# Second MLP's output GEMM by seven products instead of eight, with copied banks and stored input sums

## The chip, the cores and the metric

The kernel runs on one core of a Trainium2 chip. The metric is the device time of one execution in microseconds (us), the median of several runs. TensorE (PE) multiplies, VectorE (DVE) and ScalarE (ACT) do the elementwise work, GpSimd (POOL) and SyncE (SP) mostly issue DMAs. SBUF is the on-chip memory, PSUM the eight banks into which PE accumulates.

## What is computed

```
x = attention(q, k, v)          # keys and values averaged over 8 positions; 4608 tokens x 512
h = x @ w_in;  g = min(relu(0.5 h + 0.5)^2, 1) max h;  y = g @ w_out           # first MLP, 2048 wide
out = (sigmoid(y @ w_gate) * (y @ w_val)) @ w_out2                              # second MLP, 1536 wide
```

All in fp32. Each fp32 operand is split into a high part (fp32r, a cast) and a low part (the value minus the high part), and a product is three matmuls: high by high, high by low, low by high (`three`, L578 to L582).

## The kernel before, in words

Tokens are worked on in nine blocks of 512. The first MLP takes the nine blocks in turn; the attention of the next block runs between its matmuls. The second MLP takes block 0 alone (L797 to L826) and then four pairs of blocks (L829 to L937). A pair has a gate stage: six steps i, in each n = 0 (gate) and n = 1 (value), and for each of these twelve a 2 x 2 block product of weights (256 x 512) with inputs (512 x 1024) by Strassen's scheme in Winograd's form, seven products (`product`, L882) of six matmuls 128x512 each instead of eight. Two blocks of the seven weight matrices come from sums that block 0 computes and writes to DRAM (`prepare`, L730); a pair loads all seven of one (i, n) in one DMA of 1792 KB (`load_seven`, L765) into one of three buffers (`wa`, `wa`, `wb`). The input sums T1 to T4 are computed at the start of each pair (L852 to L870: four subtractions `minus` and seven splits for each of two halves).

Products land in four PSUM banks A to D; DVE adds (`add`, L890) combine them with SBUF copies, and `finish` (L897) applies the sigmoid or multiplies. The result `gs` (24 of 128x512 a pair) is the left operand of the output GEMM (`out_part`, L779): for each of two blocks, twelve steps m of twelve matmuls, each step split on ACT (L781) and DVE (L782), against weights that stay in SBUF (`w2`, twelve `win` buffers). `out_rows` (L592) copies the four accumulator banks out and stores.

The order on every engine is made at build time. Each operation has an engine, a cost and a key, which is a due time; `Plan.issue` (L132) walks a model of the engines and takes, among operations that could start at nearly the same time, the one with the lowest key. Keys are no earliest times: an operation goes as soon as its data and buffers are there. On the chip each engine follows the resulting order and waits on semaphores. SP's DMAs are issued in one order too.

Of the kernel before, what the change touches and what calls it, by code (L numbers as in the profile page):

```python
# [8 lines left out]
F32 = mybir.dt.float32  # L9
# [9 lines left out]
P = 128  # L19
# [45 lines left out]
class Plan:  # L65
# [7 lines left out]
    def op(self, eng, cost, key, fn, r=(), w=(), after=(), behind=(), nbytes=0, share=1.0, dmas=1):  # L73
# [24 lines left out]
        o.data, o.order = data, order - data  # L98
# [98 lines left out]
def pooled_attention_two_mlps(  # L197
# [46 lines left out]
    one, att, two = ExitStack(), ExitStack(), ExitStack()  # L244
# [50 lines left out]
    def due2(j, m):  # L295
        return due1(NB * M1 + 2) + S2 * (j * M2 + m)
# [372 lines left out]

    pools2 = {}  # L670

    def second_a():
        att.close()
        pools2["wa"] = two.enter_context(tc.tile_pool(name="wa", bufs=2))

    def second_b():
        one.close()
        pools2["right"] = two.enter_context(tc.tile_pool(name="two", bufs=1, side="right"))

    open_a = op("none", 0.0, 0.0, second_a, behind=att_ops)  # L680
    open_b = op("none", 0.0, 0.0, second_b, behind=one_ops)

    def late(tag, bufs, shape, dtype=F32, fifo=True):

        b = Buf(lambda: pools2["wa" if tag == "wa" else "right"], tag, bufs, shape, dtype, fifo)
        b.behind = [open_a if tag == "wa" else open_b]
        return b
# [5 lines left out]
    def buf_win(behind):  # L693
        b = Buf(win_p, "win", M1, [P, 2, TB], F32R)
        b.behind = behind
        return b
# [12 lines left out]
    PSTEP = 11 * 2.6  # L709
# [55 lines left out]
    def load_seven(n, i, key):  # L765
        sl, d = buf_seven(), seven[2 * i + n]
        op2(SP, 0.475, key, lambda: nc.sync.dma_start(
            out=sl.t.rearrange("p s k f -> p (s k f)").bitcast(F32), in_=d.t), r=[d], w=[sl], nbytes=P * 2 * NMAT * HK * 4)
        return sl
# [9 lines left out]
    def out_part(gs, m, key, accs, last, ahead=5):  # L779
        g = buf_g()  # L780
        op2(ACT, 0.62, key - ahead, lambda: nc.scalar.copy(out=g.t[:, 0], in_=gs.t), r=[gs], w=[g])  # L781
        op2(DVE, 0.69, key - ahead + 1, lambda: nc.vector.tensor_tensor(  # L782
            out=g.t[:, 1], in0=gs.t, in1=g.t[:, 0].bitcast(F32), op=ALU.subtract), r=[gs, g], w=[g])
# [6 lines left out]

    def buf_gs():
        return late("gs", 12, [P, TB], fifo=False)
# [9 lines left out]
    accs = [bank("acc") for _ in range(4)]  # L802
    for i in range(MP):
        slots = [prepare(n, i, due2(0, 2 * i) - 6 + 2.6 * n) for n in range(2)]
        T = due2(0, 2 * i)
        banks = {(n, f): bank("ha"[n], True) for n in range(2) for f in range(2)}
        for n in range(2):
            sl, a21 = slots[n]
            for f in range(2):
                last = []  # L810
                for c in range(KD):
# [5 lines left out]
                    last = [op(PE, 0.65, T + 5.2 * n + 2.6 * f + 0.1 * c, mm, r=[sl, a21, xs[c]], w=[banks[n, f]], behind=last)]  # L817
        for f in range(2):
            m = 2 * i + f
            t, gs = Buf(t_p, "t", 2, [P, TB]), buf_gs()  # L820
            op(ACT, 0.6, T + 2.6 * f + 5, lambda t=t, pg=banks[0, f]: nc.scalar.activation(out=t.t, in_=pg.t, func=AF.Sigmoid),
               r=[banks[0, f]], w=[t])
            op2(DVE, 0.69, T + 2.6 * f + 6, lambda t=t, gs=gs, pv=banks[1, f]: nc.vector.tensor_tensor(
                out=gs.t, in0=pv.t, in1=t.t, op=ALU.mult), r=[t, banks[1, f]], w=[gs])
            out_part(gs, m, due2(0, m) + 2 * S2 + 5.2, accs, lasts)
    out_rows(due2(0, M2 + 1) + 6, out[0:TB, :], accs)  # L826


    for pr in range(NPR):  # L829
        j1, j2 = 1 + 2 * pr, 2 + 2 * pr  # L830
        T0p = PAIR0 + PSTEP * MP * pr
        Tx = T0p - 4
# [19 lines left out]
        for kt in range(2):  # L852
            x_raw(B11[kt], 1, j1, kt, Tx - 20 + 0.1 * kt)
        for kt in range(2):
            x_raw(B22[kt], 0, j2, kt, Tx - 19 + 0.1 * kt)
            x_raw(B22[kt], 1, j2, 2 + kt, Tx - 19 + 0.1 * kt)
        for kt in range(2):
            x_raw(T4[kt], 1, j1, 2 + kt, Tx - 18 + 0.1 * kt)
        for kt in range(2):
            b11, t1, t2, t3, t4, b22 = (x[kt] for x in (B11, T1, T2, T3, T4, B22))  # L860
            u1 = minus(lambda b=b22: b.t[:, 0], lambda b=b11: b.t[:, 1], Tx + 0.1 * kt, [b22, b11])
            x_split(b11, Tx + 1 + 0.1 * kt)
            u2 = minus(lambda b=b22: b.t[:, 1], lambda b=u1: b.t, Tx + 2 + 0.1 * kt, [b22, u1])
            split_u(u1, t1, Tx + 7 + 0.1 * kt)
            u4 = minus(lambda b=t4: b.t[:, 1], lambda b=u2: b.t, Tx + 3 + 0.1 * kt, [t4, u2])
            split_u(u2, t2, Tx + 4 + 0.1 * kt)
            split_u(u4, t4, Tx + 9 + 0.1 * kt)
            u3 = minus(lambda b=b22: b.t[:, 1], lambda b=b22: b.t[:, 0], Tx + 5 + 0.1 * kt, [b22])
            split_u(u3, t3, Tx + 6 + 0.1 * kt)
            x_raw(B21[kt], 1, j1, 2 + kt, Tx - 17 + 0.1 * kt)  # L870
            x_split(B21[kt], Tx + 8 + 0.1 * kt)
            x_split(b22, Tx + 10 + 0.1 * kt)

        gss = {}
        for i in range(MP):
            sig = {}
            for n in range(2):
                T = T0p + PSTEP * i + PSTEP / 2 * n
                H = PSTEP / 14
                sl = load_seven(n, i, T - 24)  # L880

                def product(pos, o, mat, xx, start, sl=sl):  # L882
                    def mm():
                        for k in range(2):
                            ks = slice(k * P, k * P + P)
                            three(o.t, sl.t[:, 0, mat, ks], sl.t[:, 1, mat, ks], xx[k].t[:, 0], xx[k].t[:, 1],
                                  start and k == 0, k == 1, not start)
                    op(PE, 1.3, T + H * pos, mm, r=[sl] + xx + ([] if start else [o]), w=[o])
# [8 lines left out]
                def finish(key, fi, b, u):  # L897
# [7 lines left out]
                    else:  # L905
                        s, g = sig[fi], buf_gs()
                        gss[fi[1], 2 * i + fi[0]] = g
                        if u:
                            add(key, g, b, u)
                        op2(DVE, 0.69, key + 0.5, lambda: nc.vector.tensor_tensor(  # L910
                            out=g.t, in0=(g if u else b).t, in1=s.t, op=ALU.mult), r=[s, g] if u else [s, b], w=[g])

                A, Bk, Ck, Dk = bank("h", True), bank("a", True), bank("h", True), bank("a", True)
                s1 = Buf(f_p, "f", 3, [P, TB])
                u2, u3 = (late("u", 3, [P, TB]) for _ in range(2))
# [4 lines left out]
                product(2, Ck, 5, T3, True)  # L920
                add(T + H * 3, u3, Ck, u2)
                product(3, Dk, 3, T1, True)
                finish(T + H * 4, (1, 1), Dk, u3)
                product(4, A, 1, B21, False)
                finish(T + H * 5, (0, 0), A, None)
                product(5, Ck, 2, T4, False)
                finish(T + H * 6, (1, 0), Ck, u2)
                product(6, Dk, 6, B22, False)
                finish(T + H * 7, (0, 1), Dk, u2)

        for b in range(2):
            accs = [bank("acc") for _ in range(4)]
            for m in range(M2):
                out_part(gss[b, m], m, T0p + PSTEP * (3.4 + (M2 * b + m) / 4), accs, lasts, 40)
            j = j1 + b
            out_rows(T0p + PSTEP * (3.4 + (M2 * b + M2) / 4) + 1, out[j * TB:(j + 1) * TB, :], accs)

# [32 lines left out]
```

## Time and profile before

| | |
|---|---|
| median of 3 runs | 1756.0 us (1752.55 to 1757.51) |
| the profiled execution | 1755.67 us, of which the traced span is 1753.8 us |
| PE busy | 1723.8 us, 98% of the span |
| DVE busy | 1051.5 us, 60% |
| ACT busy | 805.7 us, 46% |
| DMA | 234.37 MB, mean 134 GB/s |

Busy is time in which an engine has an instruction in work; PE's matmuls are pipelined, so each is recorded as 389 ns while the next starts 227 ns after it. A wait is named after what ended it. "PEclk" is the TensorE clock granted, as a share of full speed. DMA share is the time of the packets as a share of sixteen DMA engines; packets that overlap can bring it above 1.

### The profile page before, as it was taken

To read this page: it belongs to the slowest core of one execution; us is meant where nothing else is said; L and a number is where in the kernel's file an instruction comes from. 1 tells how busy PE (TensorE), PEld (TensorE's weight loads), DVE (VectorE), ACT (ScalarE), POOL (GpSimd) and SP (SyncE) were. 2 spreads that over 40 slices of the span, in tenths; PEclk is the share of its full clock that TensorE was granted. 3 is DMA by queue.
4 is the path that set the end of the run, shared out by engine and by line. 5 is a ranking of instruction groups with operands and counts; after the bars stand their busy time and mean duration, and the time that the engine had idled before them with its cause. 6 is when DMAs were issued, how large, how long until landed. Compare 5 with 4: busy or idle time off the path is not lost.

```text
span 1753.8 us, 24039 instructions
## 1 busy us (share of the span) xinstructions
PE 1723.8 (98%) x9016; PEld 1393.4 (79%) x9016; DVE 1051.5 (60%) x1874; ACT 805.7 (46%) x1786; POOL 52.7 (3%) x90
## 2 busy tenths in 40 slices
PE   7899999999999999999999999999999999999998
PEld 5676777778777778777887888888888888888887
DVE  5899867677776867574646645345444644464432
ACT  5876656566665656564755332123222312141212
POOL 0000001010010101010000000000000000000000
PEclk9999999999999999999999999999999999999999
DMA  7742525243443414031415875354344433443411
GB/s 205 229 119 69 149 57 163 62 134 97 116 116 92 134 45 134 16 128 40 174 39 202 318 291 204 126 192 145 126 146 166 149 119 146 166 167 126 150 43 49
DMA packets 148532, 234.37 MB, mean 134 GB/s; under 512 B 84160, under 2 KB 104640, under 8 KB 140736
## 3 DMA queue, kind: packets, MB, share of 16 engines
q1 hardware_dynamic: 138624, 182.50, 33.1%
q0 software_dynamic: 9792, 50.34, 7.9%
q8 instruction: 71, 1.16, 0.3%
q14 instruction: 45, 0.37, 0.1%
HBM read 173.02 MB, written 50.33 MB: 127 GB/s over the span
## 4 chain that ended last, share of the span: by engine, by line
PE 92%; DMA 3%; DVE 2%; ACT 1%; SPq 0%; issue 0%; DVEq 0%; ACTq 0%
PE acc L580 13%; PE h L580 13%; PE acc L582 13%; PE acc L581 13%; PE h L582 13%; PE h L581 12%; PE a L582 4%; PE a L581 4%; PE a L580 4%; PE a L484 2%; DMA raw<-in_moe_w_out_dram 1%; PE a L413 1%; DMA kv<-in_v_dram 1%; DMA x<-in_v_dram 1%; DMA xb<-y 0%
## 5 line engine op out<-in xcount | busy, mean ns | idle before, releaser
L580 PE MATMUL h<-x,win 128*128 128x512 f32 x576 | 231.2, 401 | 1.0 <-ACT win L505 1.0
L580 PE MATMUL acc<-g,wj 128*128 128x512 f32 x576 | 228.7, 397 | 1.2 <-ACT g L505 1.2
L582 PE MATMUL acc<-g,wj 128*128 128x512 f32 x576 | 225.4, 391 | 3.5 <-DVE wj L514 3.5
L582 PE MATMUL h<-x,win 128*128 128x512 f32 x576 | 225.7, 392 | 1.3 <-DVE win L514 1.3
L581 PE MATMUL acc<-g,wj 128*128 128x512 f32 x576 | 225.6, 392 | 1.0 <-DVE g L514 1.0
L581 PE MATMUL h<-x,win 128*128 128x512 f32 x576 | 225.5, 391 | 0.0
L781 ACT CAST g<-gs 128x512 fp32r<-128x512 f32 x108 | 66.8, 622 | 319.2 <-PE acc L582 200.4
L645 ACT ACTIVATE t<-h,half 128x512 f32<-128x512 f32 x144 | 99.2, 689 | 186.9 <-PE h L582 186.9
L582 PE MATMUL acc<-win,g 128*128 128x512 f32 x432 | 168.2, 389 | 2.1 <-DVE g L782 2.1
L580 PE MATMUL acc<-win,g 128*128 128x512 f32 x432 | 168.2, 389 | 0.0
L581 PE MATMUL acc<-win,g 128*128 128x512 f32 x432 | 168.1, 389 | 0.0
L782 DVE TENSOR_TENSOR g<-gs,g 128x512 fp32r<-128x512 f32 x108 | 74.1, 690 | 135.2 <-ACT g L781 135.0
L649 DVE SCALAR_TENSOR_TENSOR t<-t,h 128x512 f32<-128x512 f32 x144 | 97.3, 676 | 90.9 <-ACT t L647 90.8
L580 PEld LDWEIGHTS h<-x,win 128*128 128x128 f32 x576 | 108.7, 189 | 35.7 <-issue 9.7
L582 PEld LDWEIGHTS acc<-g,wj 128*128 128x128 f32 x576 | 108.4, 188 | 28.4 <-DVE wj L514 5.4
L580 PEld LDWEIGHTS acc<-g,wj 128*128 128x128 f32 x576 | 108.2, 188 | 27.8 <-ACT g L505 1.7
L582 PEld LDWEIGHTS h<-x,win 128*128 128x128 f32 x576 | 108.7, 189 | 25.9 <-DVE win L514 2.5
L581 PEld LDWEIGHTS acc<-g,wj 128*128 128x128 f32 x576 | 108.3, 188 | 23.2 <-DVE g L514 1.6
L581 PEld LDWEIGHTS h<-x,win 128*128 128x128 f32 x576 | 108.8, 189 | 21.1
L514 DVE TENSOR_TENSOR wj<-wout_f,wj 128x512 fp32r<-128x512 f32 x144 | 99.0, 688 | 33.3 <-ACT wj L505 33.0
L514 DVE TENSOR_TENSOR g<-t,g 128x512 fp32r<-128x512 f32 x144 | 98.8, 686 | 33.6 <-ACT g L505 33.1
L505 ACT CAST g<-t 128x512 fp32r<-128x512 f32 x144 | 89.1, 619 | 52.5 <-DVE t L649 50.1
(212 smaller groups left out, 3231.1 us busy)
## 6 DMA issues: line engine op xcount, KB each, us to landing
wa<-seven SPq DMA_DIRECT2D x32, 1792.0 KB
wb<-seven SPq DMA_DIRECT2D x16, 1792.0 KB
seven<-wa POOLq DMA_DIRECT2D x8, 1792.0 KB, 7.4
y<-raw SPq DMA_DIRECT2D x18, 512.0 KB
w<-f POOLq DMA_DIRECT2D x36, 256.0 KB, 2.5
out_dram<-raw SPq DMA_DIRECT2D x18, 512.0 KB
win<-in_moe_w_in_dram SPq DMA_DIRECT2D x16, 512.0 KB
raw<-in_moe_w_out_dram SPq DMA_DIRECT2D x16, 512.0 KB
```

Source lines behind the costliest of these rows:

```text
L413: nc.tensor.matmul(out=scs[h].t[r0 % P:r0 % P + D, r0 // P * C:r0 // P * C + C], lhsT=qT.t[D * h:D * h + D, r0:r0 + D], rhs=kts[b % 2, p]. ...
L484: nc.tensor.matmul(out=px.t[D * h:D * h + D, lo:hi], lhsT=vps[b % 2, p].t[:, h], rhs=rhs, start=True, stop=True)
L505: ACT: (0.52, lambda: nc.scalar.copy(out=dst.t[:, 0], in_=src())),
L514: op(engs, [0.6 if e == DVE else 1.23 for e in engs], key, [lambda e=e: by[e].tensor_tensor(out=dst.t[:, 1], in0=src(), in1=dst.t[:, 0].bi ...
L580: nc.tensor.matmul(out=o, lhsT=wh, rhs=xh, start=start, stop=False, skip_group_check=more)
L581: nc.tensor.matmul(out=o, lhsT=wh, rhs=xl, start=False, stop=False, skip_group_check=more)
L582: nc.tensor.matmul(out=o, lhsT=wl, rhs=xh, start=False, stop=stop, skip_group_check=more)
L645: op(ACT, 0.69, Tg, lambda t=t, hps=hps: nc.scalar.activation(out=t.t, in_=hps.t, func=AF.Relu, bias=half.t, scale=0.5), r=[hps, half], w=[t])
L649: op(DVE, 0.69, Tg + 2, lambda t=t, hps=hps: nc.vector.scalar_tensor_tensor(out=t.t, in0=t.t, scalar=1.0, in1=hps.t, op0=ALU.min, op1=ALU. ...
L781: op2(ACT, 0.62, key - ahead, lambda: nc.scalar.copy(out=g.t[:, 0], in_=gs.t), r=[gs], w=[g])
L782: op2(DVE, 0.69, key - ahead + 1, lambda: nc.vector.tensor_tensor(out=g.t[:, 1], in0=gs.t, in1=g.t[:, 0].bitcast(F32), op=ALU.subtract), r ...
```

## The change

The output GEMM of each pair becomes a 2 x 2 block product as well: `hs[i]` holds, for step i, the rows f = 0, 1 of both blocks (two buffers of 128 x 2 x 512), and `out_pair` runs seven products of six steps with six matmuls each, 252 matmuls instead of 288. `prepare_out` makes the seven output weight matrices of each i in pair 0 and writes them to DRAM (42 DMAs of 256 KB from POOL); every product step loads its 256 KB back, into five `wo` buffers. The sums of the left operand are formed in place in `hs` (`comb`, four for each i). Results come out transposed: DVE transposes 32x32 blocks and SP stores runs of 256 B (`store`); the very last quarter is turned on PE (`store_rows`). In the gate stage one DMA for each product (256 KB, runs of 1 KB in DRAM, nine `ws` buffers) takes the place of the 1792 KB load, and ACT copies one bank into another before a product accumulates on it (`to_bank`), in place of DVE adds. The input sums of pairs 1 to 3 are formed during the pair before (`input_sums`, after steps 2 and 4), written to DRAM and loaded back. The new pools are opened once all of block 0's weight slots are done with (`open_c`).

```diff
-    PSTEP = 11 * 2.6
+    PSTEP = 10.5 * 2.6
...
-    def load_seven(n, i, key):
-        sl, d = buf_seven(), seven[2 * i + n]
+    def load_seven(n, i, mat, key):
+        w, d = late("ws", 9, [P, 2, HK], F32R), seven[2 * i + n]
         op2(SP, 0.475, key, lambda: nc.sync.dma_start(
-            out=sl.t.rearrange("p s k f -> p (s k f)").bitcast(F32), in_=d.t), r=[d], w=[sl], nbytes=P * 2 * NMAT * HK * 4)
+            out=w.t.bitcast(F32), in_=d.t.rearrange("p (s k f) -> p s k f", s=2, k=NMAT)[:, :, mat]), r=[d], w=[w], nbytes=P * 2 * HK * 4)
...
+    open_c = op("none", 0.0, 0.0, second_c, behind=[u for x in wb_slots for u in x.users])
...
+    def prepare_out(i, key):
+        a = Buf(raw_p, "raw", 2, [P, 4, HK], fifo=False)
+        sm = late("o", 2, [P, 4, HK])
...
+        comb(0, lambda: a.t[:, 1], lambda: a.t[:, 3], ALU.add)
...
+        for k in range(NMAT):
+            src, n = (a, (0, 2, 3)[k]) if k < 3 else (sm, k - 3)
+            w = buf_wo()
...
+            op2(PL, 1.0, key + 2 + k, lambda w=w, k=k: nc.gpsimd.dma_start(
+                out=seven_o[i][k].t, in_=w.t.rearrange("p s f -> p (s f)").bitcast(F32)), r=[w], w=[seven_o[i][k]], nbytes=P * 2 * HK * 4)
...
+    for i in range(MP):
+        prepare_out(i, PAIR0 + PSTEP * (0.2 + 0.6 * i))
...
+        def product(n, mat, o, start, what):
+            chain = []
+            for i in range(MP):
+                key = K0 + KP * (n + i / MP)
+                w, g = late("ws", 9, [P, 2, HK], F32R) if last and n and i % 3 else buf_wo(), buf_g() if i % 2 else late("g2", 3, [P, 2, TB], F32R)
+                op2(SP, 0.475, key - 20, lambda w=w, i=i: nc.sync.dma_start(
+                    out=w.t.rearrange("p s f -> p (s f)").bitcast(F32), in_=seven_o[i][mat].t),
+                    r=[seven_o[i][mat]], w=[w], nbytes=P * 2 * HK * 4)
...
+                def mm(w=w, g=g, i=i):
+                    for e in range(2):
+                        es = slice(e * P, e * P + P)
+                        three(o[e].t, w.t[:, 0, es], w.t[:, 1, es], g.t[:, 0], g.t[:, 1],
+                              start and i == 0, i == MP - 1, not start)
...
+        def buf_h(i):
+            if (MP * pr + i) % 8 < 2:
+                return late("gs", 4, [P, 2, TB], fifo=False)
+            return buf_win([], F32, False)
...
+            if pr + 1 < NPR and i in (2, 4):
+                input_sums(pr + 1, i // 2 - 1, T0p + PSTEP * (i + SUM0), plan.ops[-1])
...
+                def to_bank(key, src, dst):
+                    op(ACT, 0.6, key, lambda: nc.scalar.copy(out=dst.t, in_=src.t), r=[src], w=[dst])
...
                 product(0, A, 0, B11, True)
-                op(ACT, 0.6, T + H * 1, lambda s1=s1, A=A: nc.scalar.copy(out=s1.t, in_=A.t), r=[A], w=[s1])
-                product(1, Bk, 4, T2, True)
-                add(T + H * 2, u2, Bk, s1)
...
+                to_bank(T + H * 1, A, Bk)
+                product(1, Dk, 3, T1, True)
...
+                product(2, Bk, 4, T2, False)
+                to_bank(T + H * 3, Bk, Ck)
...
+                product(3, A, 1, B21, False)
+                finish(T + H * 4, (0, 0), A, None)
+                product(4, Ck, 5, T3, False)
+                finish(T + H * 5, (1, 1), Ck, u5)
+                product(5, Dk, 6, B22, False)
+                finish(T + H * 6, (0, 1), Dk, u2)
+                product(6, Ck, 2, T4, False)
+                finish(T + H * 7, (1, 0), Ck, None)
...
+        out_pair(pr, hs, T0p + PSTEP * (MP + 0.3))
```

## Rows read from the trace of the kernel before

**Rows 1.** The page's head: span, busy time by engine, clock granted in 40 slices.

```profile
span 1753.8 us, 24039 instructions
PE 1723.8 (98%) x9016; PEld 1393.4 (79%) x9016; DVE 1051.5 (60%) x1874; ACT 805.7 (46%) x1786; POOL 52.7 (3%) x90
PEclk9999999999999999999999999999999999999999
```

**Rows 2.** The waits of PE from 950 us on: waiter, releaser, us, times, longest.

```profile
PE acc L582 <- DVE g L782: 2.1, 1, 2.1
```

**Rows 3.** PE's timeline, 1020 to 1060 us: start, us recorded, line, tiles.

```profile
1024.20 0.39 PE L580 MATMUL acc<-win,g 128*128 128x512 f32 x1
...
1025.57 0.39 PE L580 MATMUL h<-x,wa 128*128 128x512 f32 x1
...
1026.92 0.39 PE L580 MATMUL a<-x,wa 128*128 128x512 f32 x1
...
1028.29 0.39 PE L580 MATMUL h<-x,wa 128*128 128x512 f32 x1
```

**Rows 4.** Busy time by stretch, pairs 0 to 2; last two columns DMA share and GB/s.

```profile
core 0: us, PE busy (x) PEld busy (x) DVE busy (x) ACT busy (x) POOL busy (x), PEclk, DMA share, GB/s
1025.57:1191.00 165.43, 165.43 (x731) 137.06 (x730) 81.09 (x123) 44.56 (x77) 0.00 (x0) 1.00 0.50 181
1191.00:1366.00 175.00, 175.00 (x773) 144.94 (x772) 82.69 (x124) 45.04 (x76) 0.00 (x0) 1.00 0.43 153
1366.00:1540.00 174.00, 174.00 (x769) 144.13 (x768) 82.32 (x125) 44.39 (x75) 0.00 (x0) 1.00 0.40 144
```

**Rows 5.** The same view of the output GEMM's matmuls alone (tile acc), from block 0 on.

```profile
1024.20:1050.00 25.80, 7.62 (x30) 1.00 0.67 253
1050.00:1075.00 25.00, 0.00 (x0) 1.00 0.59 217
```

**Rows 6.** The chain that ended last, its end: start, us, what.

```profile
1749.02 0.24 PE acc L582
1749.26 0.02 issue
1749.28 0.58 ACT raw L597
```

**Rows 7.** Groups of DVE and ACT in the pairs: busy us, mean ns, idle before.

```profile
L782 DVE TENSOR_TENSOR g<-gs,g 128x512 fp32r<-128x512 f32 x97 | 66.7, 691 | 134.1 <-ACT g L781 134.0
L891 DVE TENSOR_TENSOR u<-h,u 128x512 f32<-128x512 f32 x48 | 33.2, 692 | 26.6 <-PE h L582 26.3
L917 ACT COPY f<-h 128x512 f32<-128x512 f32 x48 | 28.2, 587 | 66.2 <-PE h L582 65.0
L781 ACT CAST g<-gs 128x512 fp32r<-128x512 f32 x97 | 60.0, 622 | 289.7 <-PE acc L582 200.4 <-DVE gs L910 88.1 <-DVE gs L823 0.8
```

**Rows 8.** Groups of 128x256 splits in block 0, and PE's 128x128 transposes.

```profile
L701 DVE TENSOR_TENSOR f<-f 128x256 fp32r<-128x256 f32 x10 | 4.2, 420 | 0.0
L700 ACT CAST f<-f 128x256 fp32r<-128x256 f32 x9 | 3.6, 400 | 0.0
L447 PE MATMUL acc<-ident,g 128*72 128x128 f32 x32 | 4.8, 293 | 0.6 <-DVE g L432 0.6
```

**Rows 9.** The page's DMA issues: queue, count, KB each, median us to landing.

```profile
wa<-seven SPq DMA_DIRECT2D x32, 1792.0 KB
wb<-seven SPq DMA_DIRECT2D x16, 1792.0 KB
seven<-wa POOLq DMA_DIRECT2D x8, 1792.0 KB, 7.4
w<-f POOLq DMA_DIRECT2D x36, 256.0 KB, 2.5
```

**Rows 10.** POOL's timeline: block 0's last write of weights to DRAM.

```profile
1016.67 0.53 POOL L761 DMA_DIRECT2D seven<-wb  x1 [6.69 <-DVE wb L706]
```

**Rows 11.** Landing times of DMAs that touch tile seven, then of those that touch w.

```profile
DMA to landing us min/median/max: 5.9/7.7/10.8
...
DMA to landing us min/median/max: 2.2/2.5/4.7
```

**Rows 12.** DMA of the whole core in 60 to 66 us: packets by size, rate, issues.

```profile
DMA packets 2368, 2.30 MB, mean 384 GB/s; under 512 B 279, under 2 KB 2323, under 8 KB 2368
...
win<-in_moe_w_in_dram SPq DMA_DIRECT2D x1, 512.0 KB
```

**Rows 13.** Stretches of block 0 with POOL's large writes; last columns DMA share, GB/s.

```profile
950.00:975.00 25.00, 25.00 (x111) 20.65 (x110) 21.32 (x38) 12.53 (x21) 1.60 (x3) 1.00 0.82 300
1000.00:1025.00 25.00, 25.00 (x112) 20.72 (x111) 13.32 (x23) 8.49 (x14) 1.60 (x3) 1.00 0.89 343
```

More of the change, by code (lines that the diff above doesn't have):

```diff
@@ L97, in op @@
         data.discard(o)
-        o.data, o.order = data, order - data
+        o.data, o.order = data, order - data - {o}
         o.issued = False
@@ L241, in pooled_attention_two_mlps @@
           "a": (ctx.enter_context(tc.tile_pool(name="ps_a", bufs=2, space=PSUM)), 2)}
-    one, att, two = ExitStack(), ExitStack(), ExitStack()
+    one, att, two, zero, zero_a = (ExitStack() for _ in range(5))
     edge = ctx.enter_context(tc.tile_pool(name="edge", bufs=1, side="right"))
@@ new lines, in pooled_attention_two_mlps, with input_sums, load, minus @@
+    SUM0 = 0.0
+    AHX = 20
+    sums_d = {(pr, n, kt): fixed(dram.tile([P, TB], F32, name=f"sum{pr}{n}{kt}"))
+              for pr in range(1, NPR) for n in ("T1", "T2", "T3", "T4") for kt in range(2)}
+    def input_sums(pr, kt, key, behind):
+        j1, j2 = 1 + 2 * pr, 2 + 2 * pr
+        a, b = Buf(raw_p, "raw", 2, [P, 2, TB], fifo=False), late("bt", 1, [P, TB])
+        a.behind = [behind]
+        def load(o, b, j, c, key):
+            op2(SP, 0.475, key, lambda: nc.sync.dma_start(out=o(), in_=y_d[j].t[c * P:(c + 1) * P, :]),
+                r=[y_d[j]] + ([b] if b.users else []), w=[b], nbytes=P * TB * 4)
+        def minus(o, x, y, key, name):
+            op2(DVE, 0.69, key, lambda: nc.vector.tensor_tensor(out=o[0](), in0=x(), in1=y(), op=ALU.subtract),
+                r=[a, b], w=[o[1]])
+            d = sums_d[pr, name, kt]
+            op2(SP, 0.475, key + 1, lambda: nc.sync.dma_start(out=d.t, in_=o[0]()), r=[o[1]], w=[d], nbytes=P * TB * 4)
+        def a0():
+            return a.t[:, 0]
+        def a1():
+            return a.t[:, 1]
+        def b0():
+            return b.t
+        load(a0, a, j1, kt, key)
+        load(a1, a, j2, kt, key)
+        load(b0, b, j2, 2 + kt, key)
+        minus((a0, a), a1, a0, key + 4, "T1")
+        minus((a1, a), b0, a1, key + 5, "T3")
+        minus((b0, b), b0, a0, key + 6, "T2")
+        load(a0, a, j1, 2 + kt, key + 7)
+        minus((a0, a), a0, b0, key + 10, "T4")
@@ L921, in pooled_attention_two_mlps @@
[L921 to L936, printed above, removed]
+                            out=g.t[:, bb], in0=g.t[:, bb] if u else b.t, in1=s.t, op=ALU.mult), r=[s, g] if u else [s, b], w=[g])
@@ new lines, in to_bank @@
+                def to_bank(key, src, dst):
+                    op(ACT, 0.6, key, lambda: nc.scalar.copy(out=dst.t, in_=src.t), r=[src], w=[dst])
+                A, Dk, Bk, Ck = bank("h", True), bank("a", True), bank("a", True), bank("h", True)
+                u5, u2 = late("u", 3, [P, TB]), late("u", 3, [P, TB])
+                product(0, A, 0, B11, True)
+                to_bank(T + H * 1, A, Bk)
+                product(1, Dk, 3, T1, True)
+                op2(ACT, 0.6, T + H * 2 + 0.6, lambda u5=u5, Dk=Dk: nc.scalar.copy(out=u5.t, in_=Dk.t), r=[Dk], w=[u5])
```

247 lines of the change are left out of this document (195 added, 52 removed).

## The prediction

> **What bounds the kernel now.** I read the page's head first: PE is busy 98% of the span and its clock is at full speed in every slice [rows 1], so of the engines only PE can set the time. The waits of PE from 950 us on come next: there is one, of 2.1 us, before 949.7 us, and none in the 799 us that follow [rows 2]. The timeline then gives the price of a matmul there. From the first product of pair 0 at 1025.57 us to the third at 1028.29 us there are twelve matmuls [rows 3], so one takes 2.72 / 12 = 0.2267 us and a product of six 1.36 us. A pair has 504 matmuls in its gate stage and 288 in its output GEMM, 792 x 0.2267 = 179.5 us. In the stretches of pairs 0 to 2, PE is busy all the time, DVE for 47 to 49% and ACT for 26 to 27%, and the DMA engines for 40 to 50% at 144 to 181 GB/s [rows 4]. Nothing but the count of matmuls sets the time of the pairs; a change there is worth what it takes off that count, less what it makes PE wait.
>
> **What is removed.** 288 matmuls become 252 in each of four pairs: 4 x 36 x 0.2267 = 32.6 us, all of it on the path. The profiled execution took 1755.67 us, 0.3 us below the median, so I sum against 1755.67: it goes to 1723.0 if nothing is lost.
>
> **Pair 0 without output work.** In the kernel before, pair 0 starts among the last steps of block 0: 30 output matmuls, 6.8 us, lie behind 1024.2 us, and from 1050 to 1075 us there is none while PE stays full [rows 5, 4]. So the gate stage alone keeps PE full already.
>
> **The end.** Before, the last matmul starts at 1749.02 us, the copy starts 0.26 us later and the span ends at 1753.8 us [rows 6, 1]. Now two DVE adds of 0.69 us and PE's transposes stand between; an add is 0.69 us and a copy out of PSUM 0.59 us [rows 7], and four transposes are at most 4 x 0.29 = 1.2 us by their recorded length [rows 8]. Some of the transposes overlap; the final store is half as large. I take +2.2 us, bounds +1.4 and +3.5.
>
> **DVE and ACT.** Operations per pair, counted in the diff. DVE before: 22 for inputs, 84 in the gate stage, 24 splits, 130 in all or 90 us. DVE after: 22 for inputs, 48 in the gate stage, 42 splits, 24 sums of the left operand, 6 adds, 8 transposes, 150 in all or 104 us, of a pair of 171 us: 60%. ACT: 14 + 72 + 42 + 12 = 140 at 0.61 us [rows 7], 85 us, 50%. Neither becomes the bound over a pair. The closest stretch is the last pair's output GEMM, 57.1 us of PE alone: DVE has 36 splits, 24 sums, 4 adds and 6 transposes to do in it, 70 x 0.69 = 48 us. With six `g` buffers it may run up to six steps ahead, so I take +0.5 us, bounds 0 and 5.
>
> **Copied banks.** A copy from bank to bank has no row; the nearest is the copy from PSUM to SBUF, 0.587 us. It starts 0.26 us after the start of the last matmul before it [rows 6], and one product of 1.36 us stands between. Need: 0.26 + 0.59 + about 0.05 = 0.90 us; available: 0.23 + 1.36 = 1.59 us. One other ACT operation of 0.62 us in the way costs nothing, two cost 0.5 us. The same holds for the DVE add that frees C before the last product. There are three such places in each of 48 sequences, 144. I take 0.5 us, bounds 0 and 144 x 0.15 = 22 us (the second means two operations in the way at three places in ten).
>
> **Opening the new pools.** The first `ws` load now waits for block 0's last write to DRAM, where a slot was free before. That write, one of those of 1792 KB [rows 9], is issued at 1016.67 us [rows 10]; such writes land in 5.9 to 10.8 us [rows 11], so at 1023 to 1028 us, and a load of 256 KB about as long as a write of that size, 2.5 us: the first product can start at 1026 to 1031 us. The 6.8 us of block 0's output matmuls cover PE until 1031. I take +0.5 us, bounds 0 and 5 (if those matmuls wait for their own splits).
>
> **DMA in pair 0.** Here the change piles up traffic. Each product needs 0.262 MB in 1.36 us, 193 GB/s. `prepare_out` adds 12 loads and 42 POOL writes, 54 x 0.262 = 14.2 MB, `input_sums` 4.2 MB, block 0's output 1 MB; with 22.0 MB for the gate stage that is 41.4 MB in 121 us, 342 GB/s. What the engines can do with runs of 1 KB is shown at 60 to 66 us: 384 GB/s with nearly all packets under 2 KB [rows 12]. On average it fits, but keys hold nothing back: the splits go as soon as DVE is free. For one i, DVE needs 11 x 0.42 = 4.6 us [rows 8] and has some 70% free, so 6.6 us, in which 2.36 MB move: 357 GB/s on top of 193. For some 45 to 60 us the engines are overbooked, and how they divide decides. If by bytes, the gate stage gets 192 of the 193 GB/s it needs and loses nothing; up to eight loads stand ahead as well. If packet by packet (1 KB of SP's against 2 KB of POOL's), it gets 128 of 384 GB/s; the 14.2 MB last 55 us, the gate stage does 37 us of work in that time and loses 18 us. No stretch of the trace has both queues full with such packets. I take the side of bytes with a part of the other, +4 us, bounds 0 and 18.
>
> The Trainium skill, "DMA: Bandwidth & Descriptors", Queues, rings and completion order, says that each DMA engine takes turns between its queues, a packet at a time. By that alone the sum would have 18 us in this place and come out at 1745; no row here shows the turns between these two packet sizes.
>
> **Later pairs.** 22.0 MB gate weights, 11.0 output weights, 3.7 inputs, 4.2 sums, 2.1 stores: 43 MB in 171 us, 251 GB/s against 384. SP issues some 170 DMAs of 0.3 to 0.45 us. The inputs of the next pair are loaded into buffers that come free in the order in which they are needed; the pair's last six gate products (8.2 us) and then its output GEMM cover the loads and splits: 0.
>
> Sum: 1755.67 - 32.6 + 2.2 + 0.5 + 0.5 + 0.5 + 4 = 1730.8, **1731 us**.
>
> **Rivals.** *Packets in turn* (above): PE waits on `ws` in pair 0 only, 1745 us. For it: 0.82 to 0.89 of the DMA engines were in use in block 0 with POOL's large writes [rows 13]; against: five `wo` buffers let POOL's writes hold each other back.
>
> *Short cover*: the bank copies come late because ACT does twice the work (85 us against 45). 22 us at the upper bound, 1749 us. For: idle time of ACT is spread in small pieces; against: the order is made with the copies in it, and other products can be put between.
>
> *Late output weights* (slower): five `wo` buffers must cover a load. In a stretch of output products alone a buffer comes round every 5 x 1.36 = 6.8 us, of which the product takes 1.36 and issue with handoffs 0.4, so a load may take 5.0 us. The 256 KB writes land in 2.5 us [rows 9] and at most 4.7 [rows 11]; the 1792 KB writes took 5.9 to 10.8. If a load takes 7.7 us among the others, each of 144 steps on `wo` (the last pair puts 24 of its 42 on `ws`) loses 2.7 / 5 = 0.54 us, 78 us: 1731 + 78 = 1809 us. It ends slower than before from 5.0 + 5 x 25 / 144 = 5.9 us a load. Against it: the engines are at two thirds of their rate, and before the last pair gate products stand between output steps.
>
> The Trainium skill, same page, Bandwidth, asks for DMAs of 1 MiB and more; the change goes from 1792 KB to 256 KB. The 512 KB load in runs of 1 KB that moved at 384 GB/s [rows 12] speaks against reading it as a loss here, as long as several are under way.
>
> *The matmuls don't go away*: 252 can be counted in the diff, and the seven weight sums are made once. I give it no chance.
>
> **How the numbers follow.** Forecast (1722 to 1740) 0.68; packets in turn 0.14 (1740 to 1750); short cover 0.09 (1738 to 1752); late output weights 0.09 (1735 to 1810). A measurement can tell 0.3%, 5.3 us: faster is below 1750.7, slower above 1761.3. Faster: 0.68 + 0.13 + 0.08 and a little of the last, 0.89 + 0.01; same 0.04; slower 0.06. The range from 1722 (nothing lost) to 1748 leaves out the forecast's own misses below, half of late weights and a part of short cover, under 2 in 10.
>
> **What would show it.** Right: 1008 output matmuls where there were 1152 in the pairs; PE's waits from 950 us on under 12 us in total, nearly all in pair 0 and on DMA `ws`; mid-pair DMA share about 0.7; the last pair's output stretch at 57 to 60 us. Wrong: waits on `wo` in the stretches of output products alone (late weights), many waits of 0.1 to 0.6 us on ACT's copies (short cover), or a drop of the granted clock after long waits.

## The result, and the profile after

The changed kernel takes **1727.8 us** (median of four, 1725.8 to 1729.8) against 1756.0 us, a ratio of 0.9844 [0.9831, 0.9858]: 28.2 us faster, where 25 were forecast. The profiled execution is the fastest of the four, 1725.78 us. One execution each of e1 (its profiled one) and e6 below ran at a granted clock of 0.85 and took about 150 us longer; no figure here uses them.

The page after, its head and its DMA issues (queue, count, KB each, median us to landing where the page has it):

```profile
span 1724.0 us, 25625 instructions
PE 1692.8 (98%) x8880; PEld 1364.4 (79%) x8880; DVE 1112.1 (65%) x2015; ACT 950.4 (55%) x2065; POOL 75.8 (4%) x134
PEclk9999999999999999999999999999999999999999
...
ws<-seven SPq DMA_DIRECT2D x336, 256.0 KB
...
seven_o<-wo POOLq DMA_DIRECT2D x42, 256.0 KB, 5.6
```

Against [rows 1]: PE is as full as before, at full clock, with 31 us less to do. 9016 - 144 + 8 transposes = 8880, so the 144 matmuls are gone. DVE has 61 us more work and ACT 145 us, and neither shows in the time. The 48 loads of 1792 KB of [rows 9] are 336 loads of 256 KB.

The waits of PE from 950 us to the end, the view of [rows 2] (waiter, releaser, us in total, times, longest):

```profile
PE h L582 <- DVE wa L713: 1.4, 1, 1.4
PE acc L580 <- DMA wo<-seven_o: 0.9, 2, 0.7
PE acc L580 <- ACT g L717: 0.7, 1, 0.7
PE a L580 <- DMA ws<-seven: 0.5, 1, 0.5
...
PE a L580 <- ACT a L1165: 0.4, 1, 0.4
PE h L580 <- ACT h L1165: 0.4, 1, 0.4
```

All waits together are 4.9 us, where 12 would still have borne out the forecast. The first lies ahead of the pairs. What is left is spread over output weights, a split, one gate load, two bank copies and the transposes at the end; no cause stands out.

Busy time by stretch, the view of [rows 4] (PE, PEld, DVE, ACT, POOL, granted clock, DMA share, GB/s): pair 0, then a stretch in the middle and the last pair's output stretch.

```profile
1050.00:1075.00 25.00, 25.00 (x112) 20.55 (x111) 15.63 (x34) 14.40 (x32) 7.55 (x14) 1.00 1.03 365
1075.00:1100.00 25.00, 25.00 (x112) 20.71 (x111) 16.82 (x36) 14.99 (x34) 7.02 (x14) 1.00 1.05 389
1100.00:1125.00 25.00, 24.50 (x108) 19.57 (x107) 15.06 (x29) 10.22 (x21) 4.30 (x8) 1.00 1.06 388
1350.00:1400.00 50.00, 50.00 (x223) 41.39 (x222) 22.77 (x35) 21.78 (x40) 0.00 (x0) 1.00 0.76 236
1656.50:1717.50 61.00, 60.27 (x266) 49.40 (x264) 46.63 (x74) 29.07 (x49) 0.00 (x0) 1.00 0.65 182
```

In pair 0 the DMA engines are full at 365 to 389 GB/s (217 from 1050 to 1075 before [rows 5]), and PE still misses only 0.5 us of these 75. In the last pair's output stretch DVE is busy 46.6 of 61.0 us (76%), and PE misses 0.7 us, the wait on a split by ACT (`g` L717) above.

The last pair's output matmuls alone (tile acc; PE, PEld, DVE, ACT, clock, DMA share, GB/s), and below it the end of PE's timeline (start, us, what), which answers to [rows 6]:

```profile
1656.50:1717.60 61.10, 57.51 (x252) 47.23 (x252) 3.25 (x5) 6.90 (x12) 1.00 0.65 181
```

```profile
1717.25 0.39 PE L582 MATMUL acc<-g,ws 128*128 128x512 f32 x1
...
1718.42 0.98 PE L934 MATMUL h<-id,raw 128*128 128x128 f32 x7 [0.29 <-DVE raw L910]
1719.44 0.59 ACT L938 COPY raw<-h 128x512 f32<-128x512 f32 x1 [8.82 <-PE h L934]
...
1720.16 0.91 SPq L941 DMA_DIRECT2D out_dram<-raw  x2
```

252 matmuls are busy for 57.5 us, 0.4 over 252 x 0.2267 = 57.1. The stretch of 61.1 us also holds 14 gate matmuls, 3.2 us, so the output stretch is 57.9. From the last output matmul's start to the span's end it is 1724.0 - 1717.25 = 6.75 us against 1753.8 - 1749.02 = 4.78: +2.0 us.

How POOL's 42 writes of `prepare_out` ran (duration, first and last start; then their time to landing), and the two queues' traffic from 1060 to 1100 us (packets, MB, share of the 16 engines; q1 is SP's, q0 POOL's):

```profile
L872 POOL DMA_DIRECT2D seven_o<-wo x42: 540/540/545, 1035.2 to 1110.9; - x42
...
DMA to landing us min/median/max: 4.1/5.6/7.4
```

```profile
q1 hardware_dynamic: 8713, 9.44, 67.4%
q0 software_dynamic: 1826, 5.97, 37.2%
```

In these 40 us POOL moved 149 GB/s and SP 236. The writes took 76 us.

**Where the time went.** The matmuls on the first MLP's hidden weights are not touched by the change. Their line at L580, before and then after:

```profile
L580 PE MATMUL h<-x,win x576: 389/389/628, 39.9 to 920.3; 128*128 128x512 f32 x192
L580 PE MATMUL h<-x,win x576: 389/389/794, 38.5 to 916.8; 128*128 128x512 f32 x192
```

From the last of them to the end it was 1753.8 - 920.3 = 833.5 us before and is 1724.0 - 916.8 = 807.2 now: 26.3 of the 32.6 us. The end took 2.0. From 1026 us to the last output matmul PE waited for nothing before; now its recorded waits there are 3.0 us. By the distances between the starts of its matmuls in the trace they cost 5.4 us, because a wait is counted only from a matmul's recorded end, 0.16 us after the next could have started, and the matmuls right behind a wait start late too. Before 1026 us, in block 0, PE lost 0.9 us less than before. The profiled pair differ by 3.5 us more ahead of that point, in work that the change does not touch; the other profiled executions used here reach it between 917.0 and 922.3 us. So the forecast's 25 us stand against 26.3 here, and the rest of the profiled difference is not the prediction's.

### The profile page after: what moved, and what is told of

Same layout as the page of the kernel before. It is cut to its first block, busy times and chain, and to the rows that moved or that the text cites. A ratio compares the mean times of both kernels' runs of the same rounds, so it can differ in the third digit from the quotient of the medians.

```text
span 1724.0 us, 25625 instructions
## 1 busy us (share of the span) xinstructions
PE 1692.8 (98%) x8880; PEld 1364.4 (79%) x8880; DVE 1112.1 (65%) x2015; ACT 950.4 (55%) x2065; POOL 75.8 (4%) x134
## 4 chain that ended last, share of the span: by engine, by line
PE 89%; DMA 6%; DVE 3%; ACT 1%; SPq 1%; issue 0%; DVEq 0%; ACTq 0%
PE h L580 13%; PE h L582 12%; PE h L581 12%; PE acc L580 12%; PE acc L581 12%; PE acc L582 12%; PE a L580 4%; PE a L581 4%; PE a L582 4%; PE a L484 2%; DMA raw<-in_moe_w_out_dram 2%; PE a L413 1%; DMA q<-in_q_dram 1%; DMA wo<-seven_o 1%; DMA seven<-wb 1%; DMA ws<-seven 0%
## 5 line engine op out<-in xcount | busy, mean ns | idle before, releaser
L580 PE MATMUL h<-x,win 128*128 128x512 f32 x576 | 231.0, 401 | 0.4 <-ACT win L505 0.4
L580 PE MATMUL acc<-g,wj 128*128 128x512 f32 x576 | 228.4, 397 | 1.2 <-ACT g L505 1.2
L718 DVE TENSOR_TENSOR g<-win,g 128x512 fp32r<-128x512 f32 x126 | 85.9, 688 | 106.3 <-ACT g L717 106.0
L580 PEld LDWEIGHTS h<-x,win 128*128 128x128 f32 x576 | 108.5, 188 | 35.0 <-issue 9.7
L582 PEld LDWEIGHTS acc<-g,wj 128*128 128x128 f32 x576 | 108.1, 188 | 28.7 <-DVE wj L514 5.8
L580 PEld LDWEIGHTS acc<-g,wj 128*128 128x128 f32 x576 | 108.1, 188 | 27.8 <-ACT g L505 1.7
L717 ACT CAST g<-win 128x512 fp32r<-128x512 f32 x126 | 78.2, 624 | 93.5 <-PE acc L582 80.4
L582 PEld LDWEIGHTS h<-x,win 128*128 128x128 f32 x576 | 108.5, 188 | 26.3 <-DVE win L514 3.1
L580 PE MATMUL acc<-g,wo 128*128 128x512 f32 x288 | 112.4, 390 | 1.7 <-DMA wo<-seven_o 0.9
L580 PE MATMUL h<-x,ws 128*128 128x512 f32 x288 | 112.3, 390 | 0.4 <-ACT h L1165 0.4
L581 PE MATMUL acc<-g,wo 128*128 128x512 f32 x288 | 112.1, 389 | 0.0
```

What stands on the lines that cost most here:

```text
L580: nc.tensor.matmul(out=o, lhsT=wh, rhs=xh, start=start, stop=False, skip_group_check=more)
L581: nc.tensor.matmul(out=o, lhsT=wh, rhs=xl, start=False, stop=False, skip_group_check=more)
L582: nc.tensor.matmul(out=o, lhsT=wl, rhs=xh, start=False, stop=stop, skip_group_check=more)
L717: op2(ACT, cost, key, lambda: nc.scalar.copy(out=out_hi(), in_=val()), r=[src, b], w=[b])
L718: op2(DVE, cost, key + 0.5, lambda: nc.vector.tensor_tensor(out=out_lo(), in0=val(), in1=out_hi().bitcast(F32), op=ALU.subtract), r=[src, ...
```

## The experiments

The theory is the prediction's: the count of matmuls sets the time, and the rest is hidden by buffers and order. Differences to the changed kernel are differences of the ratios to the kernel before, times 1755 us, counted from 0.9844; each is good to 3 to 5 us. A part of such a difference can lie ahead of the changed work, as above. So the table also gives, from the one trace of each kernel, what PE loses in the pairs: the time between the starts of its matmuls, from 1026 us to the last output matmul, beyond 0.2267 us for each. The kernel before loses nothing there. The profile of e1 gives no such figure.

| kernel | time against the changed kernel, us | PE's loss in the pairs, us |
|---|---|---|
| changed kernel | 0 | 5.4 |
| e5_changed_again | +0.5 | 3.4 |
| e2_six | -11.6 | 14.8 |
| e10_six_spread | -15.8 | 5.7 |
| e3_sums_at_start | +11.6 | 13.0 |
| e7_copies3 | +4.9 | 6.6 |
| e4_gate_adds, e11_gate_adds_again | +3.0, +2.6 | 6.4, 7.0 |
| e6_wo3 | +24.2 | 25.2 |
| e8_pool2 | +30.5 | 30.6 |
| e9_pool_pair2 | +29.0 | 32.5 |
| e12_pool_spread | +4.6 | 4.5 |

Each edit is built anew, so the order of the instructions can change with it: in the traces PE's order is the changed kernel's in e5, and another one in e3, e6, e7, e8, e9 and e12.

**e5_changed_again**: the changed kernel once more.

> The changed kernel itself, as the reference for the runs beside it: 1724 to 1731 us, with PE waiting under 6 us in total from 950 us on.

1728.2 us, 0.9847 [0.983, 0.9864]. The result repeats. PE's waits from 950 us on are 3.7 us, under the 6 expected.

### Does the count of matmuls set the time?

**e1_eight**: product 0's matmuls issued twice, 144 more.

```diff
+                    for r in range(2 if n == 0 else 1):
                         for e in range(2):
```

> The changed kernel, with the matmuls of each output product 0 issued twice: 288 output matmuls a pair again, all else as changed; the doubled product is counted twice in the output. Theory (the count of matmuls alone sets the time): 4 x 36 x 0.2267 = 32.6 us more than the changed kernel, 1760 us, a ratio to before of 1.00. Rival (DVE, ACT or DMA already hold PE up in the output stretches, so that extra matmuls fill gaps): under 25 us more.

0.0197 x 1755 = +34.6 us; ratio to the kernel before 1.0041 [1.0024, 1.0058]. The theory's 32.6 us is borne out: with the old count back, all that the change brought is gone.

**e2_six**: product 4 keeps two of six matmuls. The text on record has five of the six left out, 120 in all; the edit leaves out four, 96 in all, which is 21.8 us.

```diff
+                        if n == 4:
+                            nc.tensor.matmul(out=o[e].t, lhsT=w.t[:, 0, es], rhs=g.t[:, 0], start=False, stop=i == MP - 1, skip_group_check=True)
...
```

> The changed kernel, with five of the six matmuls of each step of output product 4 left out (the fifth of the seven products is incomplete); loads, splits and sums stay. Theory (PE's count alone): 4 x 30 x 0.2267 = 27.2 us less than the changed kernel, 1700 us, and no new waits of PE. Rival (DVE is next in line: 48 us of operations in the last pair's output stretch, which shrinks from 57 to 50 us): under 20 us less, with waits of PE on DVE there.

0.9778 [0.976, 0.9796], -11.6 us: half, which by its size is the rival's side (under 20). But the rival's waits on DVE did not come. PE's waits from 950 us on (us, times, longest):

```profile
PE acc L905 <- DMA wo<-seven_o: 3.5, 6, 1.1
PE acc L580 <- ACT g L717: 2.0, 3, 0.7
```

They are on output weights and on splits by ACT. A step of two matmuls lasts 0.45 us, less than the split of its operand (0.62 us on ACT, then 0.69 on DVE [rows 7]), and its weights still come through the same five buffers. PE's loss in the pairs grows by 9.4 us, about what is missing of the 21.8. Time taken off in one place outruns the supply there, so I spread it.

**e10_six_spread**: 93 matmuls left out, one from each of most steps of products 1 to 6.

```diff
+                        if n in (2, 3, 4, 5) and e == 0 and not (start and i == 0) and i < MP - 1 or n in (1, 6) and e == 0 and i in (2, 3):
...
```

> The changed kernel with one matmul left out of most steps of output products 1 to 6 (a part of the low-by-high terms is missing): 93 matmuls fewer in all, as many as in the run with a thinned product 4, which kept two of six matmuls in each step and so left out 96, not 120. Theory (that run lost half of its gain because five weight buffers could not feed steps of 0.45 us): spread out, 93 x 0.2267 = 21 us less than the changed kernel, at least 17. Rival (another engine or the DMA stands close behind PE in all output stretches): 12 us less or fewer.

0.9754 [0.9737, 0.977], -15.8 us of 21.1, between the two figures and nearer the theory's. Waits on `wo` fall to 1.5 us. In its trace PE's loss in the pairs is 5.7 us against 5.4, so there 20.8 of the 21.1 us are saved. This profiled execution spent 3.3 us more than the changed kernel's ahead of block 0 and 2.8 more in it, where nothing was changed. So by the trace the count is worth its full price downward too, as long as it is spread; by the ratio alone 5 us of that stay open.

### The zero for the later pairs

**e3_sums_at_start**: the input sums of every pair at its own start, from loaded inputs, as in the kernel before; `input_sums` is not called.

```diff
-        if pr == 0:
+        if True:
...
-            if pr + 1 < NPR and i in (2, 4):
+            if False:
```

> The changed kernel, but pairs 1 to 3 form their input sums at their own start as pair 0 does; nothing is kept in DRAM and 48 DMAs of 256 KB are gone. Theory (output products cover the boundary): within 2 us of the changed kernel. Rival (the sums at the boundary make the first gate products wait, which is what storing them avoids): 2 to 6 us for each of three boundaries, 6 to 18 us more, as waits of PE on the splits of x, win or xb.

0.991 [0.9892, 0.9928], **+11.6 us**, which is the rival's side: storing the sums is worth about 4 us at each of three transitions by the time, and 2.5 by PE's loss in the pairs (13.0 us against 5.4). Three stretches of this kernel (columns as above):

```profile
1150.00:1200.00 50.00, 47.51 (x206) 38.08 (x205) 34.66 (x57) 26.74 (x49) 0.00 (x0) 1.00 0.72 218
1300.00:1350.00 50.00, 47.32 (x203) 38.70 (x202) 37.16 (x59) 26.93 (x48) 0.00 (x0) 0.97 0.84 249
1500.00:1550.00 50.00, 48.22 (x210) 38.99 (x209) 37.90 (x62) 28.89 (x52) 0.00 (x0) 1.00 0.79 232
```

PE idles 2.5, 2.7 and 1.8 us in them; the changed kernel's PE is full in all three. In the first, DVE is busy 34.7 us against 30.4 there. PE's waits there are on a bank copy (1.5 us), an output weight (0.5) and an SBUF copy (0.4). In the second stretch it waits 2.7 us for one output weight, in the third 1.5 us for a split of the left operand. None is on the inputs themselves, which the rival had named: ACT is late with other work (in the first, the chain that ended last has it splitting an input right before the bank copy), and what held that output weight up is not shown.

### Short cover

**e7_copies3**: each bank copy made three times, 192 copies more, 109 us of ACT.

```diff
-                    op(ACT, 0.6, key, lambda: nc.scalar.copy(out=dst.t, in_=src.t), r=[src], w=[dst])
+                    for _ in range(3):
+                        op(ACT, 0.6, key, lambda: nc.scalar.copy(out=dst.t, in_=src.t), r=[src], w=[dst])
```

> The changed kernel with each copy from bank to bank made three times in a row. A copy took 0.57 us; need 0.26 + 3 x 0.57 + 0.05 = 2.0 us against 1.59 us between the products. Theory (the cover has 0.7 us to spare and no more): 0.4 us short at each of 96 copies, up to 40 us more, less where another product can be put between; at least 10 us. Rival (the order of products hides it, covers don't matter): under 4 us more.

0.9872 [0.9855, 0.9888], +4.9 us, between the rival's 4 and the theory's 10; PE's loss in the pairs grows by 1.2. PE's waits on the copies (us, times, longest):

```profile
PE a L580 <- ACT a L1166: 1.0, 2, 0.6
...
PE h L580 <- ACT h L1166: 0.6, 1, 0.6
```

Three copies take 1.7 us and the product between them 1.36, yet three waits show, not 96: other products come in between. The order was built with the three copies in it and is not the changed kernel's, so this shows that an order can be found that hides them, and not that the changed kernel's own order would.

**e4_gate_adds** and **e11_gate_adds_again**: the gate stage's old order with SBUF copies and DVE adds, all else as changed.

```diff
-                to_bank(T + H * 1, A, Bk)
-                product(1, Dk, 3, T1, True)
...
+                product(1, Bk, 4, T2, True)
+                add(T + H * 2, u2, Bk, s1)
```

> The changed kernel with the gate stage's old order of products and DVE adds in place of the bank copies on ACT. DVE gets 36 operations more a pair, 186 x 0.69 = 128 us of 171. Theory (PE's count alone, covers long enough either way): within 2 us of the changed kernel. Rival (DVE was full without the copies): 5 us or more above it, with waits of PE on DVE in the stretches of output products.

> The kernel with DVE adds in the gate stage once more, in more rounds, since the first timing could not tell 3 us from none. Theory (covers are long enough either way): within 2 us of the changed kernel, a ratio to before of 0.984 to 0.986. Rival (DVE needs the copies on ACT): 0.9865 or more.

0.9861 [0.9838, 0.9883] and 0.9859 [0.984, 0.9879]: +3.0 and +2.6 us, inside the intervals both times. The first lies between the theory's 2 us and the rival's 5, the second just inside the theory's range of ratios. The bank copies are worth 0 to 5 us by the time and 1 to 2 by PE's loss in the pairs; whether they are worth anything stays open. DVE does 1199 us of work in e4 and still does not bound it.

### Late output weights

**e6_wo3**: three `wo` buffers instead of five.

```diff
-        pools2["wo"] = two.enter_context(tc.tile_pool(name="wo", bufs=5, side="right"))
+        pools2["wo"] = two.enter_context(tc.tile_pool(name="wo", bufs=3, side="right"))
...
```

> The changed kernel with three output weight buffers in place of five. In output products alone a buffer then comes round every 3 x 1.36 = 4.1 us, and a load may take 4.1 - 1.36 - 0.4 = 2.3 us. Theory (late output weights is a real limit that five buffers just cover; a load takes 3 to 4 us among the others): 0.2 to 0.5 us for each of some 100 steps, 20 to 50 us more, as waits of PE on wo. Rival (a load lands within 2.5 us, or gate products fill in): under 5 us more.

0.9982 [0.997, 0.9994], **+24.2 us**: nearly all of the gain. The largest waits of PE, POOL's writes of `prepare_out`, and two stretches:

```profile
PE acc L580 <- DMA wo<-seven_o: 7.7, 7, 2.2
PE a L580 <- ACT x L712: 2.4, 1, 2.4
PE h L581 <- DVE x L713: 2.0, 2, 1.8
```

```profile
L872 POOL DMA_DIRECT2D seven_o<-wo x42: 540/540/545, 1038.2 to 1139.9; - x42
```

```profile
1125.00:1150.00 25.00, 23.01 (x96) 18.20 (x96) 17.14 (x30) 13.10 (x27) 3.79 (x7) 0.96 0.98 333
1150.00:1175.00 25.00, 21.54 (x82) 16.38 (x81) 14.51 (x24) 14.70 (x26) 0.00 (x0) 0.91 0.95 332
```

*Late output weights* is real: PE waits 7.7 us on them where the changed kernel waits 0.9, and five buffers are what hides it. By the prediction's working three buffers allow a load 3 x 1.36 - 1.76 = 2.3 us instead of 5.0. But the edit does a second thing. `prepare_out` works in the same buffers, and its writes now take 102 us instead of 76. In the 50 us shown, behind them, PE idles 5.5 us, 4.4 of them on splits of pair 1's inputs and 0.9 on an output weight, and the granted clock falls to 0.96 and 0.91. Of the 25.2 us that PE loses in the pairs 11.0 lie before 1200 us, where the changed kernel loses 1.9. So late output weights cost about half of the 24 us; no run separates the two.

### DMA in pair 0

**e8_pool2**: each of POOL's 42 writes made twice, the second to a scratch tensor: 42 x 256 KB = 11.0 MB more in pair 0.

```diff
+            for to in (seven_x, seven_o):
+                op2(PL, 1.0, key + 2 + k, lambda w=w, k=k, to=to: nc.gpsimd.dma_start(
...
```

> The changed kernel with POOL writing each of the 42 output weight matrices twice, the second time to a place nobody reads: 11 MB more in pair 0, whose DMA engines are already at full share for 100 us. Theory (POOL's writes hold themselves back by their five buffers, so the gate stage's loads keep what they need): under 4 us more, and the writes land later or last longer. Rival (packets in turn: with both queues full SP's 1 KB packets get a third, 128 of the 193 GB/s needed): 11 MB at 256 GB/s are 43 us more of shortage, 14 us more, as waits of PE on ws in pair 0.

1.0018 [1.0006, 1.003], **+30.5 us**, far above what was expected by either theory. Two stretches, PE's largest wait, and the two queues from 1090 to 1120 us:

```profile
1100.00:1125.00 25.00, 18.82 (x76) 13.79 (x75) 13.76 (x28) 9.70 (x22) 9.63 (x18) 0.98 1.05 402
1125.00:1150.00 25.00, 21.43 (x86) 16.16 (x85) 9.91 (x21) 10.27 (x22) 9.64 (x18) 0.95 1.04 378
```

```profile
PE h L580 <- DMA ws<-seven: 12.8, 11, 2.5
```

```profile
q1 hardware_dynamic: 5389, 6.00, 55.8%
q0 software_dynamic: 1830, 6.01, 49.4%
```

The extra bytes at the 384 GB/s of [rows 12] are 11.01 / 0.384 = 28.7 us, which is the loss within its error: pair 0 has no slack, and each further megabyte costs its own time. Both queues move 200 GB/s. From 1026 to 1200 us PE loses 28.4 us by the starts of its matmuls, where the changed kernel loses 1.9. 20.4 us are recorded as idle; about 1 is the clock (six matmuls start 0.43 us apart instead of 0.227), and the rest goes around many short waits.

**e9_pool_pair2**: the same 42 writes, of an input tile, meant for pair 2, where the engines have room. They were to follow pair 2's steps, but only the build's order said so; nothing on the chip held them, and they went out at the transition from pair 1 to pair 2. From 1300 to 1350 us the changed kernel itself moves 287 GB/s, at a DMA share of 0.91.

```diff
+            if pr == 2 and i < 5:
...
+                        out=dd.t, in_=src.t[:, 0].bitcast(F32)), r=[B11[0]], w=[dd], after=[at_], nbytes=P * 2 * HK * 4)
```

> The changed kernel with 42 writes of 256 KB from POOL (an input tile, to places nobody reads) added in steps 0 to 4 of pair 2, where the DMA engines have room: 11 MB on about 240 GB/s over some 140 us make 320 GB/s, under the 384 shown. Theory (what the same bytes cost in pair 0 was a full DMA, paid by the byte): under 4 us more. Rival (POOL's packets taking turns with SP's delay the gate loads wherever they meet): 8 us or more, as waits of PE on ws or wo in pair 2.

1.0009 [0.9998, 1.0021], **+29.0 us**. When the writes ran, the two stretches hit, finer ones of 5 us, the queues from 1341 to 1350 us, and waits from 1325 to 1376 us (waiter, releaser, us, times, longest):

```profile
L1128 POOL DMA_DIRECT2D dup<-x x42: 540/540/549, 1317.6 to 1356.0; - x42
```

```profile
1325.00:1350.00 25.00, 16.06 (x52) 10.96 (x50) 11.63 (x19) 10.60 (x19) 13.38 (x25) 0.86 1.04 410
1350.00:1375.00 25.00, 15.58 (x56) 11.90 (x57) 11.63 (x20) 5.99 (x12) 4.42 (x9) 0.86 0.97 323
```

```profile
1325.00:1330.00 5.00, 0.71 (x4) 0.25 (x2) 1.69 (x4) 1.47 (x3) 2.37 (x5) 0.94 1.04 406
1330.00:1335.00 5.00, 4.70 (x11) 3.74 (x12) 1.78 (x3) 0.86 (x2) 3.03 (x6) 0.50 1.05 414
...
1360.00:1365.00 5.00, 0.00 (x0) 0.00 (x0) 1.41 (x3) 0.00 (x0) 0.00 (x0) 0.85 0.81 267
1365.00:1370.00 5.00, 4.47 (x11) 3.50 (x12) 3.48 (x6) 2.27 (x4) 0.00 (x0) 0.50 1.00 277
```

```profile
q0 software_dynamic: 725, 2.38, 65.2%
q1 hardware_dynamic: 1218, 1.28, 39.8%
```

```profile
DVE raw L917 <- DMA out_dram<-raw: 10.9, 1, 10.9
...
PE h L580 <- DVE t L1148: 7.0, 1, 7.0
...
PE a L580 <- ACT a L1171: 4.6, 1, 4.6
...
ACT x L712 <- DMA x<-y: 4.1, 2, 2.8
```

All 42 went out in 38 us. In the burst SP's queue got 142 GB/s where a product needs 193. PE stood still from 8 us after the first write. From 1325 to 1375 us it did 108 matmuls where the price of 0.2267 us allows 220; it idled 18.4 us, and the 31.6 busy ones held matmuls worth 24.5. Of the other 7 us 4.4 are the clock: 22 matmuls start 0.43 us apart instead of 0.227.

The waits are not mainly those that the rival expected: only 2.6 us of PE's are on `ws`. The largest are on DVE and ACT, which stood behind a late DMA in their own order. ACT waited for pair 2's inputs before it came to the bank copy (4.6 us), and DVE for a store of results to leave its buffer before it came to the add of the gate stage (7.0 us). That the loss equals the bytes over the bandwidth is therefore no proof of that account here.

**e12_pool_spread**: the same 42 writes, now held on the chip by reading the result of the step that each follows (steps 0 to 3 of pair 2).

```diff
+            if pr == 2 and i < 4:
...
+                        out=dd.t, in_=src.t[:, kk % 2]), r=[hs[i][1]], w=[dd], nbytes=P * 2 * HK * 4)
```

> The changed kernel with the same 42 extra writes of 256 KB from POOL in pair 2, but really tied to the steps: 10 or 11 after each of steps 0 to 3, since each reads what that step has just finished (in the run before, nothing held them, and all went out within 39 us). Theory (extra bytes cost time only while the engines stay full for longer than the loads stand ahead, nine buffers or 12 us): four bursts of about 10 us with 15 us or more between them, under 8 us more than the changed kernel. Rival (POOL's bytes are paid in full wherever they meet SP's loads): 11 MB / 384 GB/s = 28 us more, as with the one burst.

0.987 [0.9849, 0.9891], **+4.6 us**: below the theory's 8 and far from 28. The writes, and a stretch with them:

```profile
L1188 POOL DMA_DIRECT2D dup<-win x42: 540/540/549, 1350.4 to 1446.1; - x42
```

```profile
1425.00:1450.00 25.00, 25.00 (x112) 20.67 (x112) 9.36 (x14) 9.12 (x16) 7.45 (x14) 1.00 1.05 366
```

The same bytes over 96 us leave PE full from 1300 to 1550 us, and PE's loss in the pairs is 4.5 us, no more than the changed kernel's: in this trace they cost nothing. So it isn't the bytes alone: they cost their own time where the loads have no room (e8), or when they come in one burst at a transition (e9). e12 differs from e9 in place as well as in pace, in the middle of a pair instead of at its start, and a burst in the middle was not run. No run here beats the changed kernel with the whole computation done.

## Why the prediction was right, point by point

- **What is removed** (-32.6 us): right. The 144 matmuls are gone, and e1 gives +34.6 for putting as many back.
- **The end** (+2.2): measured +2.0, by the chain foreseen: adds, transposes, copies, store.
- **DVE and ACT** (+0.5 in the last output stretch): PE's one wait there is 0.7 us, on a split by ACT, and the stretch takes 57.9 us against 57.1. DVE was to do 48 us in it; it is busy for 46.6, gate work included. Right.
- **Copied banks** (+0.5): PE's waits on them are 0.8 us. A copy from bank to bank is now a row, 0.572 us by 95 records, where 0.587 was taken from the copy to SBUF. That two operations seldom stand in the way was argued; e7 puts two more there every time and pays 5 us, not the upper bound's 22, in an order built for it. The bound left out that other products can stand between.
- **Opening the new pools** (+0.5): nothing. PE's one wait from 1025 to 1050 us, 0.37, is on a bank copy, already counted above.
- **DMA in pair 0** (+4): the term that was mis-sized, measured at 0.5 us, the one wait on `ws`. The engines are overbooked as foreseen, even for 100 us rather than 45 to 60, but the step "keys hold nothing back" failed: POOL's writes came at 149 GB/s, where seven of them in 6.6 us, as the prediction had it, are 278. Each write holds one of five `wo` buffers until it lands, 5.6 us later, which allows five writes in 5.6 us, 234 GB/s. POOL stood waiting for DVE's splits for 53 of the 76 us, and ACT's part of the splits waited 13.1 us for such a buffer. Buffers and splits paced the writes, and SP's queue kept 236 GB/s, above the 193 of a product. So the point against *packets in turn* (writes hold each other back) was the one that counted. e6 bears it out: with three buffers the same writes take 102 us. How much of the pace is the buffers' and how much the splits' is not shown. The forecast chose +4 between two ways of dividing full engines, and neither came to bear, so that its error here is only 3.5 us is partly luck.
- **Packet sizes.** The prediction put 1 KB of SP's against 2 KB of POOL's. From 1060 to 1100 us the packets average 1.1 and 3.3 KB, so turns by packet would have left SP a quarter of the rate, not a third, and the rival's price was too low.
- **Later pairs** (0): nearly right. PE waits 0.9 us on output weights there, and 0.4 on a bank copy counted above. The reason was named only as cover: it holds because the sums are stored, and without that the same cover lacks 12 us (e3).
- **Rivals.** *Late output weights*: didn't come (0.9 us), but it was the closest danger: three buffers give back 24 us, about half of it by this rival (e6), and e2 meets the same supply. *Short cover*: not near (e7). *Packets in turn*: didn't show in this kernel's time.
- **What would show it**: PE's waits stayed under 12 us, but not "nearly all in pair 0 and on DMA `ws`": that is 0.5 of 4.9 us. The 1008 output matmuls are there (252 a pair), the last pair's output stretch is at 57.9 us, and the mid-pair DMA share is 0.72 to 0.91, about the 0.7 foreseen or above it.

The Trainium skill, "DMA: Bandwidth & Descriptors", Queues, rings and completion order, has each DMA engine change queues after a packet. The runs that press both queues do not settle it: 5389 of SP's packets to 1830 of POOL's in e8, at equal bytes, and 1218 to 725 in e9, with POOL moving 1.9 times SP's bytes. Neither equal packets nor equal bytes fits both, and since no row shows whether a queue always had work, how the engines divide stays open.

More than five `wo` buffers, and fewer than nine `ws` buffers, were not tried.

## What to carry to other kernels

Where PE is full, price a change by its matmuls, then ask of each new stream how many buffers stand between its DMA and PE: here five held and three gave back nearly the whole gain. Traffic that can be done at any time was nearly free when it was paced through the middle of a pair, and cost about its bytes over the bandwidth when it was let go at once at a transition or into a full stretch; a dependency on data that comes at the right pace is a cheap way to hold it. Work on another engine that has PE's products around it can be tripled at little cost when the order is built for it (e7). Work at a transition between stages has less around it (e3). And a late DMA reaches PE through engines that work in order: in e9 a load and a store held up ACT and DVE, and these held up PE. So price a difference from the trace too, from the first matmul that the change touches: in the profiled executions here that point moves by some 5 us by itself.

## What the runs showed of the hardware that was not expected

A starved PE pays twice. In e9 it was idle for most of 1325 to 1330 us; the granted clock then was 0.50 for the next 5 us, which is the lower of its two levels (1.2 against 2.4 GHz), and 11 matmuls were done where the price of 0.2267 us allows 22. The same follows the wait from 1360 to 1365 us. Of the 25.5 us lost from 1325 to 1375, 22 matmuls that start 0.43 us apart make 4.4. In e6 eleven such matmuls in the two stretches shown make 2.2 us, beside 5.5 us of idle time.

POOL's 256 KB writes come out ahead of SP's loads of the same size when both queues are pressed and nothing holds POOL: 264 against 142 GB/s in e9. Whether SP's queue had work all the time no row shows.
